# Attention taken out of the first four expert blocks, split at an expert's end, and a fifth result tile

## The chip, the cores and the metric

The kernel runs on one core of a Trainium2 chip. The metric is device microseconds of one execution of the whole program. The core has engines that each work through their own instruction queue in order and meet only at semaphores: TensorE (PE, matrix products), VectorE (DVE), ScalarE (ACT), GpSimd (POOL) and SyncE (SP, which here issues most DMA transfers). Products are accumulated in PSUM, all other tiles lie in SBUF.

## The reference

```python
xn  = layernorm(x)                         # x: 2048 tokens of 512
out = x + A(xn) + B(xn)

# A: 32 heads of 16, each token sees itself and 7 earlier tokens, 2 apart
q, k, v = split(xn @ wqkv)
A = softmax(mask(q . k[pos - 0,2,..,14]) / 4) . v[same positions] @ wo

# B: 8 experts, each token goes to the 2 with the highest logits
gates = softmax(top2(xn @ w_gate))
B = sum over the two e of  gate_e * (silu(xn @ w1[e]) @ w2[e])   # 512 -> 1792 -> 512
```

## The kernel before

All products are made in float16 pairs: a float32 operand is split in a high part and the rest (low part), and each product is three matmuls, high by high, low by high and high by low. Hence most steps come twice: ACT makes the high part, DVE the low part.

**First phase.** The layer norm, and the products of q, k and v in four groups of 128 columns (`qkv_tile`). q, k and v are stored to DRAM. The routing (which token goes to which expert) is computed on the way. While the last two column groups run, the first attention steps are issued with them, 1.3 us of it per tile (`QATT`).

**Attention** has nothing for PE. It is done on DVE in 16 chunks (two heads each). The list `atoms` (L614 to L647) holds its steps in order, each with its cost in us written beside it: for a chunk, two products q by k (`qk`, L566) and two sums of them (`qk_sum`, L570), 2.2 each; `centre` (three short DVE steps L575 to L577 and an Exp on ACT, L578); `normal` (L583 to L585); two products with v (`pv`, L592), 2.2 each; six `fold` steps (L599); and `result` (a copy on ACT, L606, and a subtraction on DVE, L609). `load` issues the chunk's two DMAs on SP (L548, L549). Each fourth `result` also lines up four DMA transposes on SP (`turn_o`, L846). `attend(us)` (L650) adds `us` to a credit, and takes steps off the list as long as the costs handed out so far don't exceed the credit handed out so far; so one call may issue nothing, or over 4 us.

**Second phase, the experts.** Expert e (0 to 7, sorted by load) has room for `CAPS[e]` = 560, 544, 544, 512, 512, 496, 496, 480 tokens. Its 1792 hidden columns are 14 tiles of 128. The main loop (L879) has one block g for each hidden tile of each expert, 112, and 5 more. In block g:

- `up(e, f)` (L701): 12 matmuls on all its tokens, into PSUM. Experts 0 to 2 have more than 512 tokens, so a second part of 12 matmuls on 48 or 32 tokens goes to another PSUM tile with the tag `misc`, of which there is one; the main parts have two (`up`). ACT then makes Silu (L722) and the high part (L723).
- `up_low` (L726): DVE makes the low part (L729) out of the same PSUM tile. After that the tile is free for the next block.
- `down` of the block four before (`LAG` = 4): 9 matmuls into three tiles y0 to y2 (L760 to L762), and 12 into the transposed rest `yt` (L742 to L744). So blocks 0 to 3 have no `down`.
- One unit of weights, 128x1024, is split for a later block: `part_high` on ACT (L142) ahead of the products, `part_low` on DVE (L147). The unit for block g+4 is loaded by SP (`load_at`), into a staging buffer that `part_low` releases.
- `attend(EATT[...])`: 3.2 us in blocks of experts 0 to 2, 2.75 us after that, until block `att_end`.

The order of PE, ACT, DVE and SP in this loop is the order of the program text (`tc.manual_schedule`). On DVE that is: attention, `part_low`, then `up_low` of the block.

**An expert's end.** The block after its last `down` (`done` in the code; g = 18, 32, 46, ...) copies the results out. ACT: `evict` (L766) copies `yt` to a tile `yts` and y0 to y2 to three tiles `ys`. PE: `turn_y` (L779) transposes `yts` back (L787), DVE copies that to one or two more tiles (`ysr`, L791; two where an expert has over 512 tokens). SP: `store_y` (L794) writes all of them to DRAM (`yd`). The tiles `ys` and `ysr` come from one pool of four buffers (`ysp`). The next expert's first `down` writes the `yt` PSUM tiles, so it follows the copies of L791. In such a block the attention stands ahead of these copies on DVE, and `part_high` and `part_low` behind them.

**The end.** At `att_end` the attention's memory is given back. From there, step k = g - att_end: `acc` and `wo` are loaded and split (L901, L849, L854), and the rows of every token's first expert are fetched by GpSimd (L862) and added on DVE (L868). After the loop come the product with `wo` (L950 to L953), the fetch of the second expert's rows, and the output.

Of the kernel before, what the change touches and what calls it, by code (L numbers as in the profile page):

```python
# [9 lines left out]
F16 = mybir.dt.float16  # L10
# [6 lines left out]
P = 128  # L17
S = 2048
D = 512
KB = D // P  # L20
NJ = S // P
E = 8
F = 1792
FB = F // P
# [5 lines left out]
NBIG = sum(c > C0 for c in CAPS)  # L30
# [14 lines left out]
LAG = 4  # L45
FIRST = {0: (2, 3)}
WARM = 12
QATT = 1.3
EATT = (3.2, 2.75)
AHEAD = 4  # L50
NPE = 6
NDV = 2
# [4 lines left out]
def layer_kernel(ctx: ExitStack, tc, x, wqkv, wo, wg, w1, w2, out):  # L57
# [3 lines left out]
    pool = lambda n, b=1, **k: ctx.enter_context(tc.tile_pool(name=n, bufs=b, **k))  # L61
    cp = pool("cp")
# [74 lines left out]
    def part_high(kind, key, u):  # L137
        shape = [P, KB, 2, 256] if kind == 1 else [P, 2, 2, D]
        w = wsp.tile(shape, F16, name=f"w{kind}_{key}_{u}", tag=f"w{kind}")
        wgt[kind, key, u] = w  # L140
        st = staged[kind, key, u].rearrange("p (a b) -> p a b", a=shape[1])
        nc.scalar.activation(w[:, :, 0, :], st, AF.Copy, scale=SW)  # L142

    def part_low(kind, key, u):
        w = wgt[kind, key, u]
        st = staged[kind, key, u].rearrange("p (a b) -> p a b", a=w.shape[1])
        nc.vector.scalar_tensor_tensor(w[:, :, 1, :], st, SW, w[:, :, 0, :], op0=ALU.mult, op1=ALU.subtract)  # L147
# [3 lines left out]
    frp = frp_cm.__enter__()  # L151
# [19 lines left out]
            nc.sync.dma_start(t[:, c_], xv[:, 2 * g:2 * g + 2, :][:, c_])  # L171
        xg4[g] = t

    warm = cp.tile([P, D], F16, name="warm")
    nc.vector.memset(warm, 0.0)

    def warm_up(n, tag):
# [472 lines left out]
    def attend(us):  # L650
        spent[0] += us
        while atoms and spent[1] <= spent[0]:
            cost, part = atoms.pop(0)
            spent[1] += cost
            part()
# [10 lines left out]


    otp = pool("otp", reuse_waits="tile")
    ysp = pool("ysp", 4, reuse_waits="tile")
    oT = [otp.tile([P, NJ, 2, P], F16, name=f"oT_{g}") for g in range(KB)]  # L670
    mop_cm = tc.tile_pool(name="mop", bufs=2, reuse_waits="tile")
    mop = mop_cm.__enter__()
# [28 lines left out]
    def up(key, f):  # L701
        a_ = wgt[1, key, f // 2]
        fs = slice((f % 2) * P, (f % 2) * P + P)
        xt = xgt[key]
        if key == "o":
            parts = [(C0, CT, py, "misc")]
        elif key < NBIG:
            parts = [(0, C0, pu, "up"), (C0, CAPS[key], py, "misc")]
        else:
            parts = [(0, CAPS[key], py, "misc") if f in (6, 9, 12) else (0, CAPS[key], pu, "up")]  # L710
        hst[key, f] = mop.tile([P, 2, CT], F16, name=f"hh_{key}_{f}", tag="hh", bufs=LAG + 2)
        made = []
        for lo, hi, pp, tg in parts:
            ps = pp.tile([P, hi - lo], F32, name=f"pu_{key}_{f}_{lo}", tag=tg)
            for kb in range(KB):
                xh, xl = xt[:, kb, lo:hi], xt[:, KB + kb, lo:hi]
                last["pe"] = nc.tensor.matmul(ps, a_[:, kb, 0, fs], xh, start=kb == 0, stop=False)  # L717
                nc.tensor.matmul(ps, a_[:, kb, 0, fs], xl, start=False, stop=False)  # L718
                nc.tensor.matmul(ps, a_[:, kb, 1, fs], xh, start=False, stop=kb == KB - 1)  # L719
            made.append((ps, lo, hi))  # L720
        for ps, lo, hi in made:
            nc.scalar.activation(ps, ps, AF.Silu, scale=1.0 / (SW * SX))  # L722
            nc.scalar.activation(hst[key, f][:, 0, lo:hi], ps, AF.Copy, scale=SH)  # L723
        return made

    def up_low(key, f, made):  # L726
        for ps, lo, hi in made:
            hh = hst[key, f]
            nc.vector.scalar_tensor_tensor(hh[:, 1, lo:hi], ps, SH, hh[:, 0, lo:hi],  # L729
                                           op0=ALU.mult, op1=ALU.subtract)  # L730
# [35 lines left out]
    def evict(e):  # L766
        ym, yt = yacc[e]
        n = CAPS[e] - MAIN
        yts = ysp.tile([P, KB, CAPS[0] - MAIN], F32, name=f"yts_{e}", tag="yts", bufs=1)
        for h in range(2):  # L770
            nc.scalar.activation(yts[:, 2 * h:2 * h + 2, 0:n], yt[h][:, :, 0:n], AF.Copy, scale=1.0 / (SW * SH))
        out_rows = []
        for t in range(MT):
            ys = ysp.tile([P, D], F32, name=f"ys_{e}_{t}", tag="ys")
            nc.scalar.activation(ys, ym[t], AF.Copy, scale=1.0 / (SW * SH))
            out_rows.append((ys, t * P, P))
        return yts, out_rows
# [28 lines left out]
    def prep(e, t):  # L806
        if t == 0:
            new_xgt(e)
        n = tiles(e)[t]
        turn(e, t, xgt[e][:, :, t * P:t * P + n], n)  # L810
# [3 lines left out]
    def load_at(g):  # L814
        for kind, v_ in ((1, g // 2 + 2), (2, g // 2)):
            if g % 2 == kind - 1 and v_ < len(useq):
                e, u = useq[v_]
                if (1, e, 0) not in staged:
                    ereg[e] = expert_of(e)
                load_part(kind, e, ereg[e], u)  # L820
                at_block[g] = (kind, e, u)
# [27 lines left out]
    def load_wo(hf):  # L849
        st = stp.tile([P, 2, D], F32, name=f"wos_{hf}", tag="s")  # L850
        nc.sync.dma_start(st, wo.rearrange("(kb p) d -> p kb d", p=P)[:, 2 * hf:2 * hf + 2, :])
        return st

    def split_wo(hf, st):  # L854
        w = wot[:, 2 * hf:2 * hf + 2]
        nc.scalar.activation(w[:, :, 0, :], st, AF.Copy, scale=SW)
        nc.vector.scalar_tensor_tensor(w[:, :, 1, :], st, SW, w[:, :, 0, :],
                                       op0=ALU.mult, op1=ALU.subtract)

    def fetch(j, k, rows):  # L860
        yg = acp.tile([P, D], F32, name=f"yg_{j}_{k}", tag="yg")
        last["pool"] = nc.gpsimd.indirect_dma_start(  # L862
            out=yg, out_offset=None, in_=rows,
            in_offset=bass.IndirectOffsetOnAxis(ap=yrow[k][:, j:j + 1], axis=0))
        fetched[j, k] = yg

    def collect(j, k):
        nc.vector.scalar_tensor_tensor(acc[:, j, :], fetched[j, k], gord[:, k, j:j + 1], acc[:, j, :],  # L868
                                       op0=ALU.mult, op1=ALU.add)

    fetched, wos = {}, {}
    seq = [(e, f) for e in range(E) for f in range(FB)]
    att_end = (E - 1) * FB + LAG + 1
    order_cm = tc.manual_schedule(engines={mybir.EngineType.PE, mybir.EngineType.Activation, mybir.EngineType.DVE,
                                           mybir.EngineType.SP})
    order_cm.__enter__()
# [2 lines left out]
    for g in range(len(seq) + LAG + 1):  # L879
        load_at(g + AHEAD)  # L880
        done, rows = pending, None
        pending = None
        if done is not None:
            yts, rows = evict(done)
        elif g in at_block:
            part_high(*at_block[g])
        if g < att_end:
            attend(EATT[seq[g][0] >= NBIG])
        if done is None and g in at_block:
            part_low(*at_block[g])  # L890
        k = g - att_end
        if k == 0:
            assert not atoms and not turned
            atp_cm.__exit__(None, None, None)
            xgp_cm.__exit__(None, None, None)
            acp_cm = tc.tile_pool(name="acp", bufs=4, side="right")
            acp = acp_cm.__enter__()
            wot = acp.tile([P, KB, 2, D], F16, name="wot", bufs=1)
            acc = acp.tile([P, NJ, D], F32, name="acc", bufs=1)
        if 0 <= k < 4:  # L900
            nc.sync.dma_start(acc[:, 4 * k:4 * k + 4, :], xv[:, 4 * k:4 * k + 4, :])  # L901
        if 1 <= k < 3:
            wos[k - 1] = load_wo(k - 1)
        if 4 <= k < 6:
            split_wo(k - 4, wos[k - 4])
        if 2 <= k < 10:
            for j in (2 * k - 4, 2 * k - 3):
                fetch(j, 0, yd[0:ybeg(E - 1), :])
        if 3 <= k < 11:
            for j in (2 * k - 6, 2 * k - 5):  # L910
                collect(j, 0)
        if g < len(seq):
            e, f = seq[g]
            made = up(e, f)
        if done is not None:
            turn_y(done, yts, rows)
        if g < len(seq):
            up_low(e, f, made)
            if done is not None and g in at_block:
                part_high(*at_block[g])  # L920
                part_low(*at_block[g])
            if e + 1 < E and 6 <= f < 6 + len(tiles(e + 1)):
                prep(e + 1, f - 6)
            if f == FB - 3 and e + 2 < E:
                gather(e + 2)
        if LAG <= g < len(seq) + LAG:
            e, f = seq[g - LAG]
            down(e, f)
            if f == FB - 1:
                pending = e  # L930
        if done is not None:
            store_y(done, rows)
        turn_o()
# [110 lines left out]
```

## Time and profile before

| | us |
|---|---|
| median of three runs | 812.4 |
| lowest and highest | 810.68, 812.45 |
| the profiled execution | 812.17 |
| its span, first to last instruction | 810.3 |
| PE busy | 784.9 (97%) |
| DVE busy | 644.0 (79%) |
| ACT busy | 379.4 (47%) |
| mean granted TensorE clock | 0.991 |

The profile is of one execution. Lines of the timeline give the start in us from the span's start, the duration, engine, line, operation, operands and the count; in square brackets the idle time before, and what ended it. Consecutive instructions on an engine overlap a little, so the time that one costs is the distance of two starts. A table by stretches gives, for each stretch, its length, then the busy time and instructions of each engine, the granted TensorE clock (1.00 is full speed) and the DMA share and rate. The chain of waits lists, for each engine, who waited for whom: total us, times, longest.

### The profile page before, as it was taken

To read this page: it belongs to the slowest core of one execution; us is meant where nothing else is said; L and a number is where in the kernel's file an instruction comes from. 1 tells how busy PE (TensorE), PEld (TensorE's weight loads), DVE (VectorE), ACT (ScalarE), POOL (GpSimd) and SP (SyncE) were. 2 spreads that over 40 slices of the span, in tenths; PEclk is the share of its full clock that TensorE was granted. 3 is DMA by queue.
4 is the path that set the end of the run, shared out by engine and by line. 5 is a ranking of instruction groups with operands and counts; after the bars stand their busy time and mean duration, and the time that the engine had idled before them with its cause. 6 is when DMAs were issued, how large, how long until landed. Compare 5 with 4: busy or idle time off the path is not lost.

```text
span 810.3 us, 13808 instructions
## 1 busy us (share of the span) xinstructions
PE 784.9 (97%) x5318; PEld 429.0 (53%) x5318; DVE 644.0 (79%) x915; ACT 379.4 (47%) x706; POOL 99.0 (12%) x118
## 2 busy tenths in 40 slices
PE   7899999789998999999999999999999999999996
PEld 3556666445554555555555555555555555555543
DVE  7929998488996898889988898978998986356273
ACT  4643433455454636464555456455545554543100
POOL 3510402002000100010003000100100000034250
PEclk9999999979999999999999999999999999999999
DMA  8999959348454873485668547746952754494283
GB/s 288 245 290 323 312 173 246 106 132 237 159 149 148 205 208 104 172 190 168 165 203 216 155 122 225 216 125 163 297 164 87 184 137 130 143 402 115 91 275 127
DMA packets 152389, 153.89 MB, mean 190 GB/s; under 512 B 68000, under 2 KB 119456, under 8 KB 151808
## 3 DMA queue, kind: packets, MB, share of 16 engines
q1 hardware_dynamic: 147104, 136.09, 57.6%
q0 software_dynamic: 5216, 16.88, 7.2%
q8 instruction: 43, 0.70, 0.3%
q14 instruction: 26, 0.21, 0.1%
HBM read 108.12 MB, written 29.52 MB: 170 GB/s over the span
## 4 chain that ended last, share of the span: by engine, by line
PE 90%; DVE 4%; DMA 2%; issue 1%; ACT 1%; SPq 1%; POOL 0%; DVEq 0%; POOLq 0%; ACTq 0%
PE pu L719 12%; PE pu L718 12%; PE pu L717 12%; PE y L760 9%; PE y L762 9%; PE y L761 9%; PE pq L261 4%; PE pq L263 4%; PE pq L262 4%; PE yt L742 3%; PE yt L744 3%; PE yt L743 3%; PE pw L950 2%; PE pw L952 2%; PE pw L953 2%
## 5 line engine op out<-in xcount | busy, mean ns | idle before, releaser
L722 ACT ACTIVATE pu<-pu 128x512 f32<-128x512 f32 (+4 forms) x154 | 72.7, 472 | 270.5 <-PE pu L719 270.4
L717 PE MATMUL pu<-xgt,w 128*128 128x512 f16 (+4 forms) x616 | 186.4, 324 | 7.1 <-DVE hh L729 7.1
L718 PE MATMUL pu<-xgt,w 128*128 128x512 f16 (+4 forms) x616 | 186.8, 324 | 0.0
L719 PE MATMUL pu<-xgt,w 128*128 128x512 f16 (+4 forms) x616 | 182.5, 324 | 0.0
L729 DVE SCALAR_TENSOR_TENSOR hh<-pu,hh 128x512 f16<-128x512 f32 (+4 forms) x154 | 80.5, 545 | 80.9 <-ACT hh L723 80.5
L147 DVE SCALAR_TENSOR_TENSOR w<-s,w 128x1024 f16<-128x1024 f32 x112 | 136.3, 1219 | 3.9 <-ACT w L142 3.9
L762 PE MATMUL y<-w,hh 128*128 128x512 f16 x336 | 128.0, 381 | 0.0
L761 PE MATMUL y<-w,hh 128*128 128x512 f16 x336 | 127.8, 380 | 0.0
L760 PE MATMUL y<-w,hh 128*128 128x512 f16 x336 | 127.6, 380 | 0.0
L142 ACT ACTIVATE w<-s 128x1024 f16<-128x1024 f32 x112 | 116.7, 1048 | 2.9 <-DMA s<-in_B_w 2.9
L686 POOL DMA_INDIRECT xg<-xr,lis x35 | 44.7, 1277 | 496.7 <-DMA xgt<-xg 450.6
L261 PE MATMUL pq<-wq,xnT 128*128 128x384 f16 (+1 forms) x256 | 84.7, 331 | 5.4 <-DVE xnT L245 4.6
L742 PE MATMUL yt<-hh,w 128*128 128x160 f16 (+4 forms) x448 | 84.1, 223 | 3.0 <-DVE ysr L791 3.0
L718 PEld LDWEIGHTS <-w 128*128 128x128 f16 x616 | 57.8, 98 | 52.6 <-issue 9.0
L719 PEld LDWEIGHTS <-w 128*128 128x128 f16 x616 | 57.7, 98 | 52.0 <-issue 1.1
L263 PE MATMUL pq<-wq,xnT 128*128 128x384 f16 (+1 forms) x256 | 84.6, 330 | 0.0
L262 PE MATMUL pq<-wq,xnT 128*128 128x384 f16 x256 | 84.2, 329 | 0.0
L743 PE MATMUL yt<-hh,w 128*128 128x160 f16 (+4 forms) x448 | 84.0, 223 | 0.0
L744 PE MATMUL yt<-hh,w 128*128 128x160 f16 (+4 forms) x448 | 84.0, 223 | 0.0
L717 PEld LDWEIGHTS <-w 128*128 128x128 f16 x616 | 58.6, 98 | 45.1 <-issue 1.1
L723 ACT ACTIVATE hh<-pu 128x512 f16<-128x512 f32 (+4 forms) x154 | 74.6, 484 | 4.9
L592 DVE TENSOR_TENSOR pv<-kvt,at 128x2048 f32<-128x2048 f32 x32 | 72.8, 2287 | 0.4
(189 smaller groups left out, 1037.3 us busy)
## 6 DMA issues: line engine op xcount, KB each, us to landing
s<-in_B_w SPq DMA_DIRECT2D x112, 512.0 KB, 4.2
kvt<-kvd SPq DMA_DIRECT2D x16, 960.0 KB, 5.6
kvd<-ke SPq DMA_DIRECT2D x16, 512.0 KB, 4.1
yd<-ys SPq DMA_DIRECT2D x24, 256.0 KB, 2.4
xr<-xh SPq DMA_DIRECT2D x16, 256.0 KB, 4.0
qd<-qe SPq DMA_DIRECT2D x16, 256.0 KB, 3.0
qt<-qd SPq DMA_DIRECT2D x16, 256.0 KB, 4.2
acc<-in_A_x SPq DMA_DIRECT2D x4, 1024.0 KB, 15.0
```

The lines of the kernel that those rows point to most:

```text
L142: nc.scalar.activation(w[:, :, 0, :], st, AF.Copy, scale=SW)
L147: nc.vector.scalar_tensor_tensor(w[:, :, 1, :], st, SW, w[:, :, 0, :], op0=ALU.mult, op1=ALU.subtract)
L261: nc.tensor.matmul(ps[:, 0:n], xh, t[:, kb, 0:n], start=kb == 0, stop=False)
L262: nc.tensor.matmul(ps[:, 0:384], xh, t[:, kb, 400:784], start=False, stop=False)
L263: nc.tensor.matmul(ps[:, 0:n], xl, t[:, kb, 0:n], start=False, stop=kb == KB - 1)
L717: last["pe"] = nc.tensor.matmul(ps, a_[:, kb, 0, fs], xh, start=kb == 0, stop=False)
L718: nc.tensor.matmul(ps, a_[:, kb, 0, fs], xl, start=False, stop=False)
L719: nc.tensor.matmul(ps, a_[:, kb, 1, fs], xh, start=False, stop=kb == KB - 1)
L742: nc.tensor.matmul(dst, b_[:, 0, cs], hi, start=st and first, stop=False, skip_group_check=True)
L760: nc.tensor.matmul(ym[t], hi, b_[:, 0, :], start=st, stop=False)
L761: nc.tensor.matmul(ym[t], hi, b_[:, 1, :], start=False, stop=False)
L762: nc.tensor.matmul(ym[t], lo, b_[:, 0, :], start=False, stop=sp)
```

## The change

Blocks 0 to 3 get 0.7 us of attention each (`FATT`) in the place of 3.2. The other rates change little, 3.2 to 3.1 and 2.75 to 2.78. In an expert's end block, 0.4 of the block's share is handed out ahead of the result copies, and the rest behind them, after `up_low` and `part_low`. Attention may run two blocks longer (`att_end` 105 in the place of 103), and what follows it in the loop starts two blocks later. The pool `ysp` has five buffers. The tile `warm`, used for the first matmuls of all, moves to the pool of the first phase, whose memory the second phase uses again.

```diff
-EATT = (3.2, 2.75)
+EATT = (3.1, 2.78)
+FATT = 0.7
...
-    warm = cp.tile([P, D], F16, name="warm")
+    warm = frp.tile([P, D], F16, name="warm", bufs=1)
...
-    ysp = pool("ysp", 4, reuse_waits="tile")
+    ysp = pool("ysp", 5, reuse_waits="tile")
...
-    att_end = (E - 1) * FB + LAG + 1
+    att_end = (E - 1) * FB + LAG + 3
...
+        allowed = 0.0
         if g < att_end:
-            attend(EATT[seq[g][0] >= NBIG])
+            allowed = FATT if g < LAG else EATT[seq[g][0] >= NBIG]
+        now = allowed if done is None else 0.4 * allowed
+        attend(now)
         if done is None and g in at_block:
             part_low(*at_block[g])
...
             if done is not None and g in at_block:
                 part_high(*at_block[g])
                 part_low(*at_block[g])
+            attend(allowed - now)
```

## The prediction, made before the changed kernel was run

> **What bounds the kernel now.** I read the page's busy shares first, then PE's own waits, then the stretches around them.
>
> ```profile
> span 810.3 us, 13808 instructions
> PE 784.9 (97%) x5318; PEld 429.0 (53%) x5318; DVE 644.0 (79%) x915; ACT 379.4 (47%) x706; POOL 99.0 (12%) x118
> ```
> ```profile
> PE pu L717 <- DVE hh L729: 7.1, 3, 3.8
> PE yt L742 <- DVE ysr L791: 3.0, 1, 3.0
> ```
> ```profile
> 148.15:157.30 9.15, 8.56 (x61) 4.11 (x60) 3.78 (x5) 6.73 (x14) 0.00 (x0) 1.00 0.26 86
> 161.20:167.10 5.90, 5.88 (x32) 2.58 (x32) 3.96 (x7) 4.21 (x8) 0.00 (x0) 0.50 0.61 179
> 173.80:177.40 3.60, 3.60 (x18) 2.29 (x17) 3.60 (x3) 0.72 (x1) 0.00 (x0) 0.53 0.33 125
> 255.00:262.00 7.00, 4.02 (x37) 2.70 (x34) 2.41 (x5) 3.27 (x6) 0.00 (x0) 1.00 0.88 276
> 262.00:762.50 500.50, 500.50 (x3467) 270.16 (x3465) 409.51 (x447) 255.19 (x404) 40.67 (x36) 1.00 0.61 175
> 762.50:804.50 42.00, 41.51 (x205) 19.76 (x202) 22.93 (x34) 0.23 (x1) 15.89 (x16) 1.00 0.68 218
> ```
>
> PE is the bound. In the expert phase it stands still in two places only: three times (7.1 us) where `up` waits for DVE to free the one `misc` tile, and once (3.0 us) where the next expert's `down` waits for the result copies. From 262 to 762.5 it is never idle at full clock, and in the last stretch for half a microsecond. So a microsecond that PE saves before 262 arrives at the end whole, and after 262 this change has nothing to win. The first place costs more than its waits: two stretches run at 0.50 and 0.53 of the clock.
>
> How much is lost in the first place follows from PE's own starts.
>
> ```profile
> 148.15 0.38 PE L717 MATMUL pu<-xgt,w 128*128 128x512 f16 x1
> 150.74 0.19 PE L717 MATMUL pu<-xgt,w 128*128 128x48 f16 x1
> 151.04 0.38 PE L717 MATMUL pu<-xgt,w 128*128 128x512 f16 x1
> ...
> 154.38 0.18 PE L717 MATMUL pu<-xgt,w 128*128 128x48 f16 x1 [0.59 <-DVE hh L729]
> ...
> 161.22 0.20 PE L717 MATMUL pu<-xgt,w 128*128 128x48 f16 x1 [3.79 <-DVE hh L729]
> ...
> 172.64 0.18 PE L717 MATMUL pu<-xgt,w 128*128 128x48 f16 x1 [2.68 <-DVE hh L729]
> ...
> 177.46 0.38 PE L717 MATMUL pu<-xgt,w 128*128 128x512 f16 x1
> ...
> 183.21 0.38 PE L717 MATMUL pu<-xgt,w 128*128 128x512 f16 x1
> ```
>
> Block 0 takes 151.04 - 148.15 = 2.89 us (2.59 main, 0.30 `misc`), a block with `down` 183.21 - 177.46 = 5.75. Undisturbed, block 5 would start at 148.15 + 4 x 2.89 + 5.75 = 165.46; it starts at 177.46. **Lost: 12.0 us**: about 7.5 of standing still and 4.5 of half clock (half of 5.9 and of 3.6).
>
> **The change part by part.**
>
> *Blocks 0 to 3.* Which steps fall in which block follows by adding the list's costs against the credit: 32 x 1.3 = 41.6 us in the first phase, then 3.2, or now 0.7, a block. So blocks 1 to 3 got 5.1, 1.2 and 4.4 us of attention; now 0.65, 0.65 and 0.4, a single `fold` each, priced as the list has it. (Block 0's steps were done before PE reached it, either way.) The prices, from DVE and ACT:
>
> ```profile
> 154.24 2.28 DVE L566 TENSOR_TENSOR pq<-kvt,qt 128x2048 f32<-128x2048 f32 x1
> 156.44 0.69 DVE L609 SCALAR_TENSOR_TENSOR o<-ot,o 128x512 f16<-128x512 f32 x1
> 157.04 2.28 DVE L570 TENSOR_REDUCE at<-pq 128x128 f32<-128x2048 f32 x1
> 159.24 1.22 DVE L147 SCALAR_TENSOR_TENSOR w<-s,w 128x1024 f16<-128x1024 f32 x1
> 160.37 0.80 DVE L729 SCALAR_TENSOR_TENSOR hh<-pu,hh 128x512 f16<-128x512 f32 x2
> 161.08 0.42 DVE L575 TENSOR_TENSOR at<-at,mask 128x256 f32<-128x256 f32 x1
> ...
> 162.33 1.22 DVE L147 SCALAR_TENSOR_TENSOR w<-s,w 128x1024 f16<-128x1024 f32 x1
> ```
> ```profile
> 150.98 1.28 ACT L722 ACT_TABLE_LOAD   x1 [2.08 <-PE pu L719]
> 152.28 0.58 ACT L722 ACTIVATE pu<-pu 128x512 f32<-128x512 f32 x1
> 152.89 0.60 ACT L723 ACTIVATE hh<-pu 128x512 f16<-128x512 f32 x1
> ...
> 153.73 1.05 ACT L142 ACTIVATE w<-s 128x1024 f16<-128x1024 f32 x1
> 154.68 0.62 ACT L606 ACTIVATE o<-ot 128x512 f16<-128x512 f32 x1
> ```
>
> By distance of starts, DVE pays 2.20 for a `qk` or `qk_sum`, 0.60 for L609, 1.13 for `part_low`, 0.71 for `up_low`, 1.25 for the DVE half of `centre`; ACT 0.95 for `part_high`, and 1.3 from PE's end to the finished high part (0.2 to start, 0.61, 0.50). PE may write `misc` of block f+1 once `up_low` of f is done.
>
> The first wait stays: DVE had been idle, and what is late is the Silu table, 1.28 on ACT. So 154.38 stands, 0.7 by PE's starts (151.04 + 2.59 = 153.63 to 154.38). From there:
>
> - Main part of block 2 ends at 154.68 + 2.59 = 157.27. DVE: 154.24 + 0.65 `fold` + 1.13 + 0.71 = 156.7. In time.
> - Block 3's main ends at 160.15, `up_low` of 2 at 159.4 (ACT delivers at 158.6); block 4's at 163.03, `up_low` of 3 at 162.3. ACT's work per block is 0.95 + 1.45 of 2.89. In time by 0.7.
> - Block 4 now has a `fold`, `qk` and `result`: 162.3 + 0.4 + 2.20 + 0.60 + 1.13 + 0.71 = 167.3. PE has a `down` by then and needs it at 163.3 + 2.85 + 2.59 = 168.75. In time.
> - Block 5: `qk_sum` and `centre` end at 170.75, Exp 0.5 (half as wide as L723's 0.60), the Silu table 1.28, Silu and copy 1.1, `up_low` 0.75: 174.4 or later. PE needs it at 168.75 + 5.75 = 174.5. I put 0.15 of waiting.
> - Block 6: `qk` and `qk_sum` 4.40 + 1.13 + 0.71: 180.75, needed at 180.4: 0.4. Blocks 7 and 8 (`normal`, three short steps taken like those of `centre`, 1.3, and `pv` 2.2; then `pv`) end at 186.1 and 190.2, needed at 186.5 and 192.3. The debt is paid.
>
> Left of the 12.0 are 0.7 + 0.55. **Gain 10.7**; bounds: 12.0 if nothing is left, and 6.3 if one wait as at 172.64 stays with its slow stretch (12.0 - 1.25 - 2.7 - 1.8). I take 10.7, since each step has a row. No gap then exceeds 0.7, and the slow stretches go with the gaps: before each stood a gap of 2.68 or 3.79, and the 0.59 was followed by none.
>
> By the Trainium skill ("TensorE: Matmul & The Clock Gate", Part 1: The HAM clock gate), the clock halves after an idle window of some 3.4 us, with windows that run freely. The trace agrees only in part: 2.68 us sufficed at 172.64 and 2.98 us at 261.02 did not (clock 1.00 from 255 to 262); read by its letter, the second stretch isn't the gap's doing and would stay, which is rival 1.
>
> *Expert 0's end.*
>
> ```profile
> 251.12 2.28 DVE L592 TENSOR_TENSOR pv<-kvt,at 128x2048 f32<-128x2048 f32 x1
> ...
> 260.28 0.68 DVE L791 COPY ysr<-yr 48x512 f32<-48x512 f32 x1 [3.90 <-DMA yd<-ys]
> ```
> ```profile
> 253.43 0.34 SPq L549 DMA_DIRECT2D kvt<-kvd  x1
> 253.88 2.35 SPq L796 DMA_DIRECT2D yd<-ys  x3
> ```
> ```profile
> 251.28 1.64 ACT L775 ACTIVATE ys<-y 128x512 f32<-128x512 f32 x3
> ```
> ```profile
> 257.66 0.38 PE L762 MATMUL y<-w,hh 128*128 128x512 f16 x1
> 261.02 0.23 PE L742 MATMUL yt<-hh,w 128*128 128x160 f16 x1 [2.98 <-DVE ysr L791]
> ```
>
> The fifth result needs a fifth tile, and with four it waits for the first one's store, which stood on SP behind a chunk's load, itself waiting for DVE's `pv`. A 512-wide matmul holds PE for 2.59 / 12 = 0.22, so PE loses 261.02 - 257.88 = 3.14. With five tiles the store no longer matters, and the load falls in block 22. What is late next is the split: a credit of 0.4 x 3.1 lets `result` through and then the 2.2 of `qk_sum`, all ahead of the copies, so here nothing moves behind them. L606 starts after `evict`, at 251.28 + 1.64 = 252.9; L609 at 253.55; `qk_sum` 254.15 to 256.35; two copies of 0.6 to 0.7 to 257.6. PE needs them at 257.88. Bounds 0 and 3.14; **gain 2.9**, with 0.2 for a margin this thin.
>
> *Edits at nothing.* At the other ends PE doesn't wait before, so the split and the fifth tile win nothing there; blocks 32 and 46 now hold an Exp with two table loads (3.0 us) on ACT between `evict` and Silu, covered by the 2.85 us of `down` and 2.59 of the next `up` that follow before `misc` is needed; uncovered, at most 3.0 each. The moved `load`s, `result`s and transposes keep their number and come three to five blocks later on SP; the weights' DMAs queued among them run four blocks ahead of use, some 20 us, which covers them. `warm` is done long before its memory is reused. The rate 2.78 adds 2 us of DVE in all, which was busy 409.5 of 500.5 us from 262 on. The attention ends in block 101 rather than 97, `acc`, `wo` and the fetches two blocks later: rival 3.
>
> Sum: 10.7 + 2.9 = 13.6, span 796.7. The profiled run's time was 812.17, 0.2 below the median; from the median, **798.8 us**.
>
> **The rivals.**
>
> 1. *A slow stretch of the clock stays* without a long gap before it. For it: the small gaps at blocks 1, 6 and 7 remain, and 2.68 us already sufficed. Against it: from 148.15 to 157.30, with the 0.59 gap in it, the clock was 1.00. Price half of 3.6: 800.6. Chance 0.1. The same page of the Trainium skill, "TensorE: Matmul & The Clock Gate" (A second HAM failure mode: psum-queue depth-cycling), speaks for it: short idle times between groups of matmuls can make the clock swing.
> 2. *DVE's debt of blocks 5 to 7 is larger*, through Exp, for which ACT and DVE wait in turn: one full wait of 2.7 stays with its stretch, 1.8, less the 0.55 counted: 802.7. For it: the two long waits of before came behind 5.1 and 4.4 us of attention, and block 6 has 4.4. Against it: from 154.2 up to `up_low` of block 8 DVE has eight blocks of 1.13 + 0.71 and 18.5 us of attention, 33, and PE needs the last at 192.3, so 5 us of idling fit. Chance 0.1.
> 3. *Slower: the fetches become the end's bound.* The last sixteen additions of L868 now come two blocks later, ahead of expert 7's copy on DVE, and that copy ahead of its store, the second fetches and the output.
>
> ```profile
> 754.34 0.75 DVE L868 SCALAR_TENSOR_TENSOR acc<-yg,gord,acc 128x512 f32<-128x512 f32 x1 [0.63 <-DMA yg<-yd,yrow]
> 762.58 0.69 DVE L791 COPY ysr<-yr 96x512 f32<-96x512 f32 x1 [7.49 <-PE yr L787]
> 770.83 0.69 DVE L955 SCALAR_TENSOR_TENSOR rs<-pw,acc 128x512 f32<-128x512 f32 x1
> ```
>    Two blocks without `up` are 2 x (5.75 - 2.89) = 5.7 us, and 762.58 - 755.1 = 7.5 are free. Beyond that, PE has six PSUM tiles of 2.6 us (to 778) before it needs the output step of 770.83, 7 more. Only past 7.5 + 7 + 13.6, a fetch chain over 28 us late, does it end slower; at 30 us late it gives 814. Chance 0.03.
> 4. *The change doesn't do what it says at expert 0's end*: the copies are late behind `qk_sum`, and PE waits 3 us as before: 801.7. Chance 0.05. That also the first blocks don't move, 812.4: 0.02.
>
> **How the numbers follow.** The forecast, 798.8, has 0.70, with 797.3 to 800.2 of its own. All 15.1 gone gives 797.3; the runs before spread by 1.8, half of it gives 796.4. The upper end takes in rivals 1, 4 and 2: 802.7. A measurement of this kernel tells 0.3%, 2.4 us, from no change. Faster 0.95, same 0.02, slower 0.03.
>
> **What would show it.** PE's waits for L729 fall from 7.1 to about 1.2, no stretch between 148 and 190 has a clock under 0.95, block 5 starts near 166.2; the wait of L742 for L791 is gone, and L791 no longer waits for a store; PE stays full until 749. Wrong would be: waits of over 2 us at blocks 5 to 7, a DVE wait for L868 that ends last after 749, or new PE waits at blocks 32 and 46.

## The result, and the profile after

| | before | changed |
|---|---|---|
| median, us | 812.36 | 799.88 |
| lowest and highest | 810.68, 812.45 | 798.24, 800.44 |
| profiled execution, its time | 812.17 | 798.24 |
| its span | 810.3 | 796.4 |

The ratio of the times is 0.985, with a 95% interval of 0.983 to 0.987: 12.5 us, or 1.5%, faster. The page of the changed kernel's profile begins:

```profile
span 796.4 us, 13794 instructions
PE 779.9 (98%) x5318; PEld 427.2 (54%) x5318; DVE 642.4 (81%) x915; ACT 379.0 (48%) x706; POOL 105.5 (13%) x118
```

PE has the same 5318 matmuls, and DVE, the engine whose work was moved, is as busy as before (642.4 against 644.0). Nothing was saved; work was put where PE doesn't wait for it. PE's waits in the expert phase, from the same view as before (lines of the code are one higher in the changed kernel), and the table by stretches of its profile:

```profile
PE pu L718 <- DVE hh L730: 1.0, 2, 0.6
```
```profile
147.00:158.00 11.00, 10.41 (x82) 5.20 (x80) 5.08 (x9) 7.89 (x16) 0.00 (x0) 1.00 0.35 106
158.00:190.00 32.00, 31.41 (x249) 17.54 (x247) 29.36 (x36) 19.11 (x36) 2.85 (x3) 1.00 0.60 171
190.00:270.00 80.00, 80.00 (x634) 45.58 (x633) 69.88 (x84) 43.09 (x83) 7.83 (x4) 1.00 0.65 182
270.00:740.00 470.00, 470.00 (x3218) 252.87 (x3216) 395.86 (x429) 243.32 (x379) 40.58 (x32) 1.00 0.60 176
```

The three waits of 7.1 us in all have become two of 1.0, the wait for the result copies is gone, and the clock is 1.00 from 147 on. The timeline of PE gives the two waits that are left, and block 0's and block 5's first matmul:

```profile
147.35 0.38 PE L718 MATMUL pu<-xgt,w 128*128 128x512 f16 x1
...
153.58 0.18 PE L718 MATMUL pu<-xgt,w 128*128 128x48 f16 x1 [0.59 <-DVE hh L730]
...
165.40 0.38 PE L718 MATMUL pu<-xgt,w 128*128 128x512 f16 x1
...
180.39 0.18 PE L718 MATMUL pu<-xgt,w 128*128 128x48 f16 x1 [0.46 <-DVE hh L730]
```

From block 0 to block 5 it takes 18.05 us, where it took 29.31 and the undisturbed sum is 17.31. Blocks 6 and 7 take 6.03 and 6.36 us in the place of 5.75 (blocks 6, 7 and 8 start at 171.15, 177.18 and 183.54): the wait in block 6 is too short for the view of waits, and the listed 0.46 in block 7 is 0.61 by starts.

Whole times of this kernel scatter by 2 us and more from one execution to the next. A finer measure is the distance between two of PE's own starts, from the first matmul of block 0 to the first product with `wo`. It leaves out the first phase and the output. The second of these starts is, before and after:

```profile
762.37 0.38 PE L950 MATMUL pw<-wot,oT 128*128 128x512 f16 x1
```
```profile
748.08 0.38 PE L955 MATMUL pw<-wot,oT 128*128 128x512 f16 x1
```

This **expert phase** took 762.37 - 148.15 = 614.22 before, and 748.08 - 147.35 = 600.73 after: 13.49 us less. In the four profiles of this kernel and of its two variants without the split or the fifth tile (e1, e2, e5 below) it is 600.71 to 600.73, so it tells hundredths of a microsecond where the clock isn't disturbed.

### The profile page after: what moved, and what is told of

Same layout as the page of the kernel before. It is cut to its first block, busy times and chain, and to the rows that moved or that the text cites. A ratio compares the mean times of both kernels' runs of the same rounds, so it can differ in the third digit from the quotient of the medians.

```text
span 796.4 us, 13794 instructions
## 1 busy us (share of the span) xinstructions
PE 779.9 (98%) x5318; PEld 427.2 (54%) x5318; DVE 642.4 (81%) x915; ACT 379.0 (48%) x706; POOL 105.5 (13%) x118
## 4 chain that ended last, share of the span: by engine, by line
PE 91%; DVE 3%; DMA 1%; ACT 1%; issue 1%; SPq 0%; POOL 0%; DVEq 0%; POOLq 0%; ACTq 0%
PE pu L718 12%; PE pu L720 12%; PE pu L719 12%; PE y L761 9%; PE y L763 9%; PE y L762 9%; PE pq L262 4%; PE pq L264 4%; PE pq L263 4%; PE yt L743 3%; PE yt L745 3%; PE yt L744 3%; PE pw L955 2%; PE pw L957 2%; PE pw L958 2%
## 5 line engine op out<-in xcount | busy, mean ns | idle before, releaser
L719 PE MATMUL pu<-xgt,w 128*128 128x512 f16 (+4 forms) x616 | 185.3, 322 | 0.0
L687 POOL DMA_INDIRECT xg<-xr,lis x35 | 51.6, 1473 | 482.2 <-DMA xgt<-xg 434.6
```

## The experiments

Times are medians of 4 to 12 executions, each set timed beside the kernel before (its medians there are 811.97 to 812.36). "Block 0 to 5" and "expert phase" are distances of starts in the one profile of each run, as above.

| run | median us | ratio to before, 95% interval | block 0 to 5 | expert phase |
|---|---|---|---|---|
| before | 812.36 | | 29.31 | 614.22 |
| changed | 799.88 | 0.985 (0.983 to 0.987) | 18.05 | 600.73 |
| e1, changed, again | 799.23 | 0.984 (0.982 to 0.986) | 18.05 | 600.71 |
| e2, first four blocks alone | 799.57 | 0.984 (0.982 to 0.986) | 18.05 | 600.72 |
| e3, fifth tile alone | 808.58 | 0.995 (0.993 to 0.997) | 27.64 | 609.41 |
| e4, split alone | 812.99 | 1.001 (1.000 to 1.002) | 29.21 | 616.51 |
| e5, changed with four tiles | 799.72 | 0.984 (0.982 to 0.986) | 18.05 | 600.73 |
| e6, before, load behind stores | 808.74 | 0.995 (0.993 to 0.997) | 29.32 | 611.08 |
| e7, share 2.0 | 801.00 | 0.985 (0.983 to 0.987) | 20.59 | 602.35 |
| e8, Silu table and share, misplaced | 799.72 | 0.984 (0.983 to 0.986) | 18.05 | 599.92 |
| e9, Silu table and share | 796.49 | 0.981 (0.979 to 0.982) | 17.31 | 599.18 |
| e10, before, again | 812.76 | 1.000 (0.999 to 1.001) | 29.34 | 615.61 |

### e1: the changed kernel again

> The changed kernel as it is, to see what other executions do. Its timed runs were 798.2 to 800.4, with a granted clock of 0.997 in the fastest and 0.993 in the others. Theory A (the clock caught a gap of the first phase in those): the expert phase is the same in every profile, and a run near 800 shows a second slow stretch before 48 us, where PE stands still for 2.5 us near 26. Theory B (rival 1 of the prediction): the slow stretch lies between 148 and 190, behind the small gaps that are left, and the stage from block 0 to block 8 is longer by about 1.7 us.

It has no edit. Its timed executions were 798.16 to 800.19. The profile, of an execution of 798.47, has in the first phase

```profile
14.00:48.00 34.00, 30.84 (x187) 17.68 (x185) 25.19 (x68) 20.34 (x58) 16.38 (x14) 0.90 1.00 256
```

a clock of 0.90, where the first profile of the same program has 0.97, and 1.00 from 147 to 740. Block 0 starts at 147.35 in one and 147.96 in the other, while the expert phase is the same to 0.02 us. Both are among the shorter executions, so for those near 800 the variants below have to serve: the profiles of e2 and e5 (799.57 and 799.72) have a clock of 0.88 from 14 to 48, start block 0 at 149.40 and 149.46, and have the same expert phase. So what differs lies mainly ahead of block 0, as theory A has it. Theory B falls.

### e2, e3, e4: each part alone

```diff
 # e2
-            attend(EATT[seq[g][0] >= NBIG])
+            attend(FATT if g < LAG else EATT[seq[g][0] >= NBIG])    # FATT = 0.7; att_end + 2
 # e3
-    ysp = pool("ysp", 4, reuse_waits="tile")
+    ysp = pool("ysp", 5, reuse_waits="tile")                        # and warm in frp
 # e4
-            attend(EATT[seq[g][0] >= NBIG])
+            allowed = EATT[seq[g][0] >= NBIG]
+        now = allowed if done is None else 0.4 * allowed
+        attend(now)
...
+            attend(allowed - now)                                   # behind part_low
```

> Only the first four blocks are changed (0.7 in blocks 0 to 3, 3.2 and 2.75 after that, the two blocks more at the end, four result tiles, no split). Theory A, as the prediction has it: the first place gives 10.7, and with four tiles the wait at expert 0's end stays, so 801.5 and a PE wait of about 3 us on the result copies. Theory B: that wait came from a chunk's load standing on SP ahead of the stores; the moved list puts that load four blocks later by itself, so the wait is gone with four tiles too, and the time is that of the full change, 798 to 800.

> Only the fifth result tile (and the warm-up tile in the other pool). Both theories: the result copy no longer waits for a store, PE's wait at expert 0's end (3.0 us) goes, the three waits at blocks 1, 2 and 4 and the two slow stretches stay: 809.2, 3.1 under the kernel before. If the copies are late for another reason, 812.

> Only the split of the attention at an expert's end (0.4 before the result copies, the rest behind), with four tiles and the old shares. The prediction gives it nothing: block 18 keeps the product with v ahead of the copies and moves a fold and the chunk's load behind them, but on SP the load still stands ahead of the stores, so PE's 3 us wait stays: 812.3, within 0.5. If the split is what frees the copies: 809.

**The first four blocks alone give the whole of it**: 799.57, an expert phase of 600.72 against 600.73, and with four result tiles PE's waits there are one line,

```profile
PE pu L718 <- DVE hh L730: 1.0, 2, 0.6
```

without one on the result copies. SP's timeline in e2 has the load well behind the stores:

```profile
242.82 1.34 SPq L797 DMA_DIRECT2D yd<-ys  x3
247.30 0.92 SPq L797 DMA_DIRECT2D yd<-ysr  x2
...
264.50 0.34 SPq L550 DMA_DIRECT2D kvt<-kvd  x1
```

Theory B holds, and the prediction's theory A, by which 3 us would have stayed, falls. The fifth tile alone gives 808.58, as both theories had it (809.2): the wait at expert 0's end goes there too. The split alone gives nothing that can be told (1.001, and 1.000 is just in the interval); PE's wait stays, and SP's timeline in e4 shows why:

```profile
251.86 0.34 SPq L549 DMA_DIRECT2D kvt<-kvd  x1
252.31 2.44 SPq L796 DMA_DIRECT2D yd<-ys  x3
```
```profile
259.38 0.23 PE L742 MATMUL yt<-hh,w 128*128 128x160 f16 x1 [2.92 <-DVE ysr L791]
```

The load that the split put later on DVE's side of the text still stands ahead of the stores on SP. The median is 0.7 above the kernel before of its set, a little more than the 0.5 that was allowed, and the expert phase is 2.29 longer than before. The profile shows where:

```profile
259.00:265.00 6.00, 5.62 (x38) 3.09 (x38) 6.00 (x9) 0.32 (x1) 0.00 (x0) 0.72 0.71 199
```

A slow stretch follows PE's wait at expert 0's end (by starts 1.8 us; the profile of before has none there), and in block 36, at 362.45, PE waits 0.53 for L729 (by starts 0.7), a wait that no other profile here has.

### e5, e6: the tile or the load

```diff
 # e5: the changed kernel
-    ysp = pool("ysp", 5, reuse_waits="tile")
+    ysp = pool("ysp", 4, reuse_waits="tile")
 # e6: the kernel before
         if done is not None:
             store_y(done, rows)
+        while held:                    # loads that fell in this block
+            held.pop(0).load()
         turn_o()
```

> The changed kernel with four result tiles in the place of five. Theory B (from the run with the first four blocks alone): no load stands ahead of the stores any more, the first store lands before the fifth copy is due, nothing is lost: 799.5, and no PE wait on the result copies. Theory A (the fifth tile is what counts): that wait of 3 us is back, 802.5.

> The kernel before with one edit: in an expert's last block, a chunk's load that falls there is issued on SP behind the stores of the results, not ahead of them. Four tiles, the old shares, no split. Theory B: this alone ends PE's wait at expert 0's end, as much as the fifth tile did, 808.9, with the three waits at blocks 1 to 4 as before. Theory A: four tiles are still one too few, 812.3.

Both came out as theory B has it. e5's expert phase is 600.73, so in the changed order the fifth tile is worth nothing. In e6, with four tiles and the old shares, SP's and DVE's timelines at expert 0's end read

```profile
252.85 1.33 SPq L800 DMA_DIRECT2D yd<-ys  x3
257.32 0.92 SPq L800 DMA_DIRECT2D yd<-ysr  x2
258.30 0.42 SPq L552 DMA_DIRECT2D qt<-qd  x1
258.77 0.44 SPq L553 DMA_DIRECT2D kvt<-kvd  x1
```
```profile
256.61 1.28 DVE L795 COPY ysr<-yr 128x512 f32<-128x512 f32 x2 [1.15 <-PE yr L791]
```

The stores go first, the tiles are free in time, and DVE makes both copies in one go, waiting only for PE's transposes. The expert phase is 611.08, that is 614.22 - 3.14, the very length of the wait. So the wait had two conditions, one tile too few and a load ahead of the stores, and it went with either.

### e7: more attention in the first four blocks

```diff
-FATT = 0.7
+FATT = 2.0
```

> The changed kernel with 2.0 us of attention in each of the first four blocks in the place of 0.7. If the share there is what costs (DVE's work per block against PE's 2.89): a block's 2.0 + 1.13 + 0.71 = 3.8 is 1 us over, so PE waits again at two of the blocks 2 to 4, some 2.7 us together, but no gap above 2.1, so about no slow stretch: 802 (up to 804 with one). If only the gaps that halve the clock cost: within 0.5 of the changed kernel.

It came out at 801.0, with an expert phase 1.62 longer than the changed kernel's. PE's waits behind the first one:

```profile
159.73 0.18 PE L718 MATMUL pu<-xgt,w 128*128 128x48 f16 x1 [1.67 <-DVE hh L730]
166.22 0.18 PE L718 MATMUL pu<-xgt,w 128*128 128x48 f16 x1 [0.55 <-DVE hh L730]
```

By starts they cost 2.54 up to block 5 (20.59 - 18.05), where 2.7 was expected. Of that, the 0.9 that blocks 6 and 7 lose in the changed kernel has to be taken off, since they lose nothing here; there is no slow stretch. So attention costs there by its length as well, not only where it halves the clock. Whole times alone (801.0 against 799.88, in overlapping ranges) would have shown little of it.

### e8, e9: the two waits that were left

```diff
 # e8: the changed kernel
+    nc.scalar.activation(root, eps, AF.Silu)         # one column, ahead of block 0
-EATT = (3.1, 2.78)
+EATT = (3.2, 2.8)
+MATT = 2.6                                           # blocks 4 to 8
...
-            allowed = FATT if g < LAG else EATT[seq[g][0] >= NBIG]
+            allowed = FATT if g < LAG else MATT if g < LAG + 5 else EATT[seq[g][0] >= NBIG]
 # e9: as e8, but
-    nc.scalar.activation(root, eps, AF.Silu)
+    behind(nc.scalar.activation(root, eps, AF.Silu), "act")
```

> The changed kernel with two edits: a one-column Silu ahead of the first block, so that the table is loaded while ACT waits for PE (the wait of 0.6 us at block 1, 0.75 by starts), and 2.6 us of attention in blocks 4 to 8 (3.2 and 2.8 after that), to pay DVE's debt there (0.46 at block 7). If both waits have those causes, both go, and the time is 1.2 us under the changed kernel, 798.3. If the table isn't what is late, the wait at block 1 stays and 0.5 is gained at most.

> As the last version, but the one-column Silu is tied behind the last copy of the first phase; there it had been moved to the program's start, where it cost a table load ahead of the layer norm, and the wait at block 1 stayed (0.6). From the first Silu of the experts' phase to the first product with wo the changed kernel takes 597.9 us in every profile, the last version 597.1. If the table is what is late at block 1, that wait goes (0.75): 596.3 counted from the same point of PE's work, 1.5 under the changed kernel in all. If not, 597.1.

e8 missed: 799.72, no better. ACT's and PE's timelines tell why:

```profile
2.30 1.28 ACT L880 ACT_TABLE_LOAD   x1
3.60 0.20 ACT L880 ACTIVATE root<-eps 128x1 f32<-128x1 f32 x1
```
```profile
156.33 0.18 PE L719 MATMUL pu<-xgt,w 128*128 128x48 f16 x1 [0.58 <-DVE hh L731]
```

The little Silu depended on nothing, and had been put at the program's start; the table was changed again before block 0. The wait at block 7 did go, as the smaller share was to make it: the expert phase is 0.81 shorter. The median doesn't show it; the profiled execution has a late block 0, at 150.10. In e9 the Silu is tied behind the last copy of the first phase:

```profile
147.87 1.28 ACT L880 ACT_TABLE_LOAD   x1
```

With it no wait is left in the expert phase. Block 0 to 5 takes 17.31, the undisturbed sum of the prediction to the hundredth, and the expert phase 599.18, 1.55 under the changed kernel (expected 1.5). The median, 796.49, lies lower still, 3.4 under the changed kernel's; what goes beyond 1.55 lies outside the expert phase (below). To the kernel before, timed beside it, the ratio is 0.981.

### e10: the kernel before again

> The kernel before once more, for its profile. If the slow stretches of the clock are a matter of where free-running windows fall on PE's gaps, then the gaps at blocks 1, 2 and 4 and at expert 0's end are there again at the same lengths, within 0.1 where no slow stretch lies between, but the slow stretches need not lie at the same places, and the experts' phase differs from 611.4 by up to 2 us. If the stretches are bound to the gaps, they lie where they did and the phase is 611.4 within 0.1.

The gaps are at the same places: 0.59, 3.79, 3.02 (2.68 before) and 2.65 (2.98). The slow stretches behind the second and third gap are there again (0.60 from 161 to 167, 0.66 from 172 to 177), but a new one follows the fourth. In the profile of before the clock was 1.00 from 255 to 262 and full behind it. In e10:

```profile
255.00:262.00 7.00, 4.35 (x31) 2.56 (x29) 3.25 (x6) 2.77 (x5) 0.00 (x0) 0.96 0.87 267
262.00:267.00 5.00, 5.00 (x29) 2.13 (x28) 3.70 (x5) 1.46 (x5) 0.00 (x0) 0.72 0.92 240
```

So a gap at the same place, and a shorter one, brought a slow stretch here, and the expert phase is 1.39 longer. The stretches aren't bound to the gaps, as the first theory has it. That free-running windows are the reason agrees with this; no view shows the windows themselves.

## Why the prediction was right

The forecast was 798.8 with a range of 796.4 to 802.7; the median is 799.88. Point by point:

- **Blocks 0 to 3.** Forecast gain 10.7. Measured: 29.31 - 18.05 = 11.26 up to block 5, less the 0.28 and 0.61 that blocks 6 and 7 then lose: 10.4. That the first wait stays because of the Silu table is shown by e9, which differs from e8 only in where the little Silu stands, loads the table earlier, and has no wait.
- **The debt of blocks 5 to 7.** The changed kernel starts block 0 at 147.35, 0.80 earlier than before; with that taken off, `up_low` of blocks 4, 5, 6 and 7 was to end at 166.5, 173.6, 179.95 and 185.3. DVE's timeline shows the starts of what followed it:

```profile
166.51 2.27 DVE L571 TENSOR_REDUCE at<-pq 128x128 f32<-128x2048 f32 x1
...
173.89 2.28 DVE L567 TENSOR_TENSOR pq<-kvt,qt 128x2048 f32<-128x2048 f32 x1
...
180.26 0.41 DVE L584 TENSOR_REDUCE mx<-at 128x32 f32<-128x256 f32 x1
...
185.61 2.28 DVE L593 TENSOR_TENSOR pv<-kvt,at 128x2048 f32<-128x2048 f32 x1
```

  Each is met within 0.31 us, and the waits come in the two blocks where they were put, but larger: 0.15 and 0.4 became 0.28 and 0.61 by starts.
- **Expert 0's end.** Forecast gain 2.9, all but 0.2 of 3.14. Measured 3.1: the whole wait is gone. PE and DVE after:

```profile
246.50 0.38 PE L763 MATMUL y<-w,hh 128*128 128x512 f16 x1
246.72 0.23 PE L743 MATMUL yt<-hh,w 128*128 128x160 f16 x1
```
```profile
242.32 0.69 DVE L610 SCALAR_TENSOR_TENSOR o<-ot,o 128x512 f16<-128x512 f32 x1 [2.27 <-ACT o L607]
242.93 2.28 DVE L571 TENSOR_REDUCE at<-pq 128x128 f32<-128x2048 f32 x1
245.13 1.27 DVE L792 COPY ysr<-yr 128x512 f32<-128x512 f32 x2
```

  DVE does wait for L607 behind `evict`, `qk_sum` does stand ahead of the copies, and PE goes on from one matmul to the next without a gap. But **the step that named the cause was half wrong**: "with five tiles the store no longer matters, and the load falls in block 22" puts the tile first. e2 and e5 show the moved load to be enough, and the tile then idle; e3 shows the tile to be enough where the load stays. The prediction had both halves in one sentence and counted them once, so the sum came out. That it came so close, 13.6 against 13.49, is partly luck: the first place gave 0.3 less than forecast and this one 0.2 more.
- **The split.** Forecast nothing; e2, with neither split nor fifth tile, and e5, with the split alone of the two, have the same expert phase to 0.01.
- **Half clock.** The prediction divided the 12.0 lost into 7.5 of standing still and 4.5 of slow stretches. The total held; the division did not. In e3 the stretch behind block 4's gap is missing (a gap of 3.31, then a clock of 1.00 from 174.1 to 190), and block 0 to 5 took 27.64: that stretch cost 1.67. The first stretch cost nothing of its own, since PE would have waited for DVE there anyway. In e3 block 3 takes 4.90 us with a wait, before 5.52 without one, and the waits are longer in all, 8.3 in place of 7.1:

```profile
PE pu L717 <- DVE hh L729: 8.3, 4, 3.8
```

  Yet from block 2's first matmul to the end of the gap in block 4 it takes 17.96 us before (154.68 to 172.64) and 17.97 in e3 (156.07 to 174.04). So of the 12.0, half clock cost 1.7, and waiting for DVE the other 10.3, 0.74 of them through the Silu table.

- **The rivals.** A slow stretch that stays, a full wait of 2.7 through a larger debt, and a wait that stays at expert 0's end aren't in the profile. The one on the slower side, fetches that bound the end, came nearer than thought:

```profile
746.46 0.75 DVE L869 SCALAR_TENSOR_TENSOR acc<-yg,gord,acc 128x512 f32<-128x512 f32 x1 [0.24 <-DMA yg<-yd,yrow]
748.28 0.69 DVE L792 COPY ysr<-yr 96x512 f32<-96x512 f32 x1 [1.07 <-PE yr L788]
```

  DVE now waits for the fetched rows (0.24 here, 0.6 to 1.3 in the steps before), and of the 7.49 us of idling ahead of expert 7's copy 1.07 are left. The forecast left 7.5 - 5.7 = 1.8. It costs nothing that can be told: from the first product with `wo` to the end it is 48.3 us, 47.9 before, and 48.4 in e10.
- **The median.** The forecast span was 796.7 and the profiled one 796.4, but the profiled execution is the fastest of the four, and its block 0 starts 0.80 earlier than before, which is scatter of the first phase; so this closeness is luck in part. The median of the executions lies 1.1 above the forecast. The forecast moved the median of before by the gain in one profile. The expert phase gained 13.5, the medians 12.5. In the twelve profiles here block 0 starts between 146.7 and 150.1, in a phase whose order on PE no edit touched; the six with the latest start have a clock of 0.87 to 0.89 from 14 to 48, and the others 0.90 to 0.98. Why a program falls in one or the other more often (e9's five executions were all short) stays open.

## What to carry to other kernels

Where the bound engine is stalled by a helper, add up the helper's work per block against the bound engine's own time for that block: blocks at a pipeline's start, which lack part of the steady work, take less of it, and what is handed out too early there is paid at full length. A wait for a buffer has a releaser with a queue of its own; look at what stands ahead of the releasing transfer there before adding a buffer. Measure an edit in a long kernel by the distance of two of the bound engine's own starts around it, since whole times also carry the scatter of phases that the edit doesn't touch.

## What the runs showed of the hardware that was not expected

Whether a gap halves the clock is not a matter of its length alone. e3 and e4 have the same gap at block 4, and the clock behind it is 1.00 in e3 and 0.57 in e4:

```profile
174.04 0.18 PE L717 MATMUL pu<-xgt,w 128*128 128x48 f16 x1 [3.31 <-DVE hh L729]
```
```profile
174.00:177.20 3.20, 3.16 (x34) 2.09 (x34) 3.10 (x4) 1.35 (x3) 0.00 (x0) 1.00 0.49 169
```
```profile
171.18 0.20 PE L717 MATMUL pu<-xgt,w 128*128 128x48 f16 x1 [3.31 <-DVE hh L729]
```
```profile
171.00:175.00 4.00, 3.82 (x22) 1.67 (x22) 3.90 (x7) 1.35 (x3) 0.00 (x0) 0.57 0.49 135
```

Gaps of 2.65 (e10), 2.68 (before) and 3.02 (e10) were followed by slow stretches as well, and a gap of 2.98 (before) by none. That agrees with the free-running windows that the Trainium skill states ("TensorE: Matmul & The Clock Gate", Part 1: The HAM clock gate), but not with a wholly idle window of 3.4 us as the condition.

A table load on ACT can wait with the instruction that needs it, and then stands behind that wait: at block 0 the Silu table's load began only when PE's products were there (2.08 us idle ahead of it before, and again after). It isn't always so. In the changed kernel the load for the Exp in block 5 ran first, and only the Exp waited:

```profile
165.03 1.28 ACT L579 ACT_TABLE_LOAD   x1
170.20 0.42 ACT L579 ACTIVATE at<-at 128x256 f32<-128x256 f32 x1 [3.89 <-DVE at L578]
```

Why the load at block 0 waits and this one doesn't stays open. A one-column activation of the same function took the load at block 0 off PE's path when it was held in its place: 0.74 us (e9 against e8).
